# A changed order of eight MLP steps, and two splits queued behind a relu, in a fused attention and MLP kernel

## The chip, the core and the metric

The kernel runs as one program on one NeuronCore of a Trainium2 chip. Its time is the device time of one execution in microseconds. The core has five engines that run side by side and meet through semaphores: TensorE (PE, matrix products into PSUM banks), VectorE (DVE), ScalarE (ACT), GpSimd (POOL) and SyncE (SP, which issues the loads and stores). Each engine takes its own instructions strictly in the order in which they were queued, so an instruction that waits holds up all that stand behind it on that engine.

## The reference, cut to what matters

The kernel chains three blocks on a batch of 2 sequences of 768 tokens and 512 channels: an attention with decay, a token and channel mixing block, and a last block in which the change lies:

```
X = np.fft.fft(np.fft.fft(x, axis=1), axis=2)
u = x + np.real(X)
mu = np.mean(u, axis=-1, keepdims=True)
var = np.mean((u - mu) ** 2, axis=-1, keepdims=True)
un = (u - mu) / np.sqrt(var + 1e-06)
out = u + np.maximum(un @ w_ch1, 0.0) @ w_ch2     # 512 -> 2048 -> 512
```

## The kernel before

The last block works on one sequence b at a time, on halves c of 384 tokens, and on tiles f of 128 of the 2048 hidden channels. Every float32 operand is kept as a high and a low part, and each product is three matmuls (lines 138 to 140, `mm3`): high times high, high weights times low data, low weights times high data, in the order of the code.

A plain step is one pair (c, f). Its first product (`first`) is twelve matmuls of 384 columns from the normalised input `un` of that half and the weight `w_a` into a PSUM bank of the pool `ph`, which has two banks. Then the relu: ACT writes the high part of `hid` (line 515), and DVE the low part (line 516). The second product (`second`) is nine matmuls of 512 columns from `hid` and the weight `w_b` into three accumulator banks `ac`. The loop `run` issues in step i the first product of step i, then the second product of step i-1. So a relu has the second product of one step in which to be done; the third matmul of a second product is the first that reads the low part.

The list `todo` has 68 steps. Steps 60 to 67 are the eight last plain steps, all of sequence 1: tiles f = 0 to 3 of both halves. At the end of step 61, PE transposes the last two rows of tiles of sequence 1 (line 939, `pn`), ACT and DVE turn them into the high and low part of `un` of half c = 1 (lines 945 and 946). Nothing of half c = 1 can be multiplied before.

After the plain steps come groups called `seven`: for two hidden tiles and both halves they do seven half products in place of eight, from sums of weights (`w_s`, lines 241 to 244 on DVE) and sums of inputs (`tops`, `input_sums`, lines 599 to 609). The banks are `pa`, `pb` and `pc`, all from the same pool of two. `pa` is finished by the relu `hid_11`, `v` is collected by lines 657 and 661, and line 664 is the last reader of `pb`. In between, the function `between` puts second products of the group before. The input sums of sequence 1 are queued on DVE after step 61; the last of them, `input_sums_last`, overwrites a quarter of `un` of half c = 1 in place (ACT line 618, DVE line 619), so it must wait for the first product of step 67, which reads the old content.

Weights are loaded by SP into one of three `raw` buffers and split: ACT writes the high part (line 280, or 271 for sums), POOL subtracts it from the raw words for the low part (line 281, or 272). The POOL instruction frees the raw buffer for the next load. The weights of tiles 10 and up come as 64-bit words, and ACT (lines 226 and 229) and DVE (lines 249 and 254) make floats of them first. `convert` takes one such job per step; a job is taken only when weight tiles have become free.

The order on PE and SP is that of the code. The order on DVE, ACT and POOL is made by a scheduler from dependencies and its own estimate of times, except where `tc.issue_after(ins)` puts what is queued in it behind `ins` on the engine of `ins`. `urgent` holds the last relu queued on ACT and on DVE.

Of the kernel before, what the change touches and what calls it, by code (L numbers as in the profile page):

```python
# [57 lines left out]
def f32(ap):  # L58
    return ap.bitcast(F32)
# [3 lines left out]
def body(ctx: ExitStack, tc: tile.TileContext, qkv, kT, lam, w_tok1, w_tok2,  # L63
# [37 lines left out]
    urgent = {}  # L101
# [11 lines left out]
    def acc_bank(n):  # L113
        return ps_acc.tile([P, 512], F32, tag="acc", name=n)
# [7 lines left out]
    def big_tile(n, dt=F32):  # L122
        return big_p.tile([P, BIG], dt, tag="big", name=n)

    def half_tile(shape, n, dt=F32):
        return half_p.tile(shape, dt, tag="half", name=n)

    def temp(w, n, dt=F32):
        return t_p.tile([P, 2 * NQ + 2], dt, tag="t", name=n)[:, :w]
# [57 lines left out]
    def load_next():  # L187
        job = next_job()
        if job is None:
            return False  # L190
        kind, key = job
        at_["load"] += 1
        jobs.append(job)
        raw = raw_p.tile([P, 1024], U32, tag="raw", name="raw_" + "_".join(map(str, key)) + kind[0])
        raws[job] = raw
        if key[0] == "dft":
            nc.sync.dma_start(raw.bitcast(F32)[:, :512], dft[key[1]])
        elif kind == "sums":
            for i, k in enumerate(pair_keys(key)):
                nc.sync.dma_start(raw.bitcast(F32)[:, i * 512:(i + 1) * 512], singles[place_of(k)])  # L200
        elif kind == "single":
            nc.sync.dma_start(raw.bitcast(F32)[:, :512], singles[place_of(key)])
        else:
            w = {"t1": lambda: w_tok1[key[1]], "t2": lambda: w_tok2[key[1], key[2]],
                 "a": lambda: (w_ch1, m_ch1)[key[1]][key[2]], "b": lambda: (w_ch2, m_ch2)[key[1]][key[2]]}[key[0]]()
            nc.sync.dma_start(raw[:, :2 * width(key)], w)
        return True
# [179 lines left out]
    def load_qkv(b, hp):  # L387
        t = half_tile([P, 4, S], f"qkv_{b}_{hp}")
        nc.sync.dma_start(t[:, 0, :], qkv[b, hp, :, 0])
        nc.sync.dma_start(t[:, 1:3, :], qkv[b, hp, :, 1:3])  # L390
        pair[b, hp] = t

    def load_kp(b, hp, kp):
        nc.sync.dma_start(kp, kT[b, hp].rearrange("p (c j) -> p c j", j=C))
# [3 lines left out]
    def attention_scores(b, hp, dT, pw, kp):  # L398
        n = f"{b}_{hp}"
        t = pair[b, hp]  # L400
        q, kn, v, qs = (t[:, i, :].rearrange("p (c j) -> p c j", j=C) for i in range(4))
        sts = {}
        st2 = temp(4 * C, f"st2_{n}").rearrange("p (a c j) -> p a c j", a=2, c=2)
        for g, cs in enumerate((range(4), range(4, NC))):
            m = len(cs)
            ps = [(ph_bank, x_bank)[g](f"s_{n}_{g}_{a}") for a in range(2)]
            for i, c in enumerate(cs):
                for a in range(2):
                    r = slice(a * D, (a + 1) * D)
                    nc.tensor.matmul(ps[a][:, i * C:(i + 1) * C], kp[r, c, :], q[r, c, :], start=True, stop=True)  # L410
            for a in range(2):
                st = st2[:, a] if g else temp(4 * C, f"st_{n}_{a}").rearrange("p (c j) -> p c j", c=4)
                tt(out=st, in0=ps[a][:, :m * C].rearrange("p (c j) -> p c j", c=m),
                   in1=dT[:, 2 * hp + a:2 * hp + a + 1, :].to_broadcast([P, m, C]), op=ALU.mult)
                for i, c in enumerate(cs):
                    sts[c, a] = st[:, i, :]
        nc.gpsimd.tensor_tensor(
            out=qs[:, 1:, :], in0=q[:, 1:, :],
            in1=pw[:, hp:hp + 1, :].to_broadcast([P, NC - 1, C]), op=ALU.mult)
        pair[b, hp] = t, sts  # L420
# [193 lines left out]
    def input_sums_last(b, k):  # L614

        t = tops[b, 4][:, k]
        src = cores.pop((b, k))
        nc.scalar.activation(t[:, 0, :], src, AF.Copy)
        tt(out=t[:, 1, :], in0=src, in1=f32(t[:, 0, :]), op=ALU.subtract)
# [73 lines left out]
    def seconds(b, p, starts, ends):  # L693
        f = 2 * p
        return [(b, c, f_, starts and j < 2, ends and j > 1)
                for j, (c, f_) in enumerate(((0, f), (1, f + 1), (0, f + 1), (1, f)))]
# [17 lines left out]
    def units(m, blocks, last_f):  # L714
        return [(m, fs, b, c, f, f == last_f) for fs, b in blocks for c in range(2) for f in fs]
# [242 lines left out]

    todo = units(0, [(G1[0], 0), (G1[0] + G1[1], 1), (G1[1] + G1[2], 0), (G1[3], 0), (G1[2] + G1[3], 1)], 11)
    todo += units(1, [(G1[0] + G1[1], 0)], 15)  # L960
    todo += [(1, None, 1, c, f, False) for c, f in ((0, 0), (0, 1), (1, 0), (1, 1), (0, 2), (1, 2), (0, 3), (1, 3))]


    by_seven = [(b, p, p == first_p, p == ps[-1]) for b, ps, first_p in (
# [41 lines left out]
    with tc.manual_schedule(engines={ENG.SP, ENG.PE}):  # L1006
        dT, pw, kps, bds, skew = attention_setup()

        def load(n):
            load_kp(n // NP, n % NP, kps[n % NP])  # L1010
            load_qkv(n // NP, n % NP)

        load(2)
        skew(6, H)
        load(3)
        for _ in range(3):
            load_next()
        for b in range(B):
            xT[b] = big_tile(f"xT_{b}")[:, :4 * S].rearrange("p (k s) -> p k s", k=4)

        def scores(n):
            attention_scores(n // NP, n % NP, dT, pw, kps[n % NP])

        def states(n):
            attention_states(n // NP, n % NP, dT, pw)

        def result(n):
            attention_out(n // NP, n % NP, bds[n % 2], x_bank if n == 7 else acc_bank)


        warm = acc_bank("warm")

        def keep_warm(n):
            for _ in range(n):
                nc.tensor.transpose(warm[:, :P], ident, ident)

        def constants():
            rawx = temp(P, "rawx")
            nc.sync.dma_start(rawx, dft_x)
            nc.scalar.activation(cx, rawx, AF.Copy)  # L1040

        keep_warm(22)
        acts = {"s": scores, "u": states, "r": result, "l": load, "c": convert, "x": token_in, "h": token_hidden,
                "o": token_out, "m": run, "w": lambda: keep_warm(8), "k": constants}
        for word in EARLY.split():
            acts[word[0]](*(int(i) for i in word[1:]))
        run(54 - step["i"])
        free = big_tile("tops_0", F32R).rearrange("p (j k h s) -> p j k h s", j=2, k=2, h=2)
        half = half_tile([P, 2, 2, 2, HS], "tops_1", F32R)
        free = [free, big_tile("tops_2", F32R).rearrange("p (j k h s) -> p j k h s", j=2, k=2, h=2)]  # L1050
        homes = {1: (free[0][:, 0], free[0][:, 1], half[:, 0]), 0: (free[1][:, 0], free[1][:, 1], half[:, 1])}
        pieces = [input_sums(0, k, homes[0]) for k in range(2)]
        for fn in pieces[0]:
            fn()
            run(1)
        run(62 - step["i"])
        for k in range(2):
            for fn in input_sums(1, k, homes[1]):
                fn()
        run(64 - step["i"])  # L1060
        input_sums_last(0, 0)
        for fn in pieces[1]:
            run(1)
            fn()
        run(len(todo) - step["i"])
        for k in range(2):
            input_sums_last(1, k)
        pend = [(False, lambda: second(todo[-1]))]

        place = {"i": 0}  # L1070

        def between():
            j, i = divmod(place["i"], 4)
            place["i"] += 1
            turns = TURNS_7[j] * (i + 1) // 4 - TURNS_7[j] * i // 4
            ends, fn = pend.pop(0) if pend else (False, lambda: None)
            if ends:
                fn()
            convert(turns)
            if not ends:  # L1080
                fn()

        for j, u in enumerate(by_seven):
            seven(u[0], u[1], between)
            last = j == len(by_seven) - 1
            todo_ = seconds(*u)
            if last:
                for x in (todo_[0], todo_[2]):
                    second_of(*x)
                second_two(todo_[1], todo_[3])  # L1090
            else:
                pend.extend([(x[4], lambda x=x: second_of(*x)) for x in todo_])
            if j == 0:
                input_sums_last(0, 1)
# [99 lines left out]
```

## Time and profile before

| | us |
|---|---|
| median of 3 runs | 611.98 |
| lowest and highest | 611.23, 612.0 |
| the profiled execution | 612.37 |
| its span, first to last instruction | 610.6 |

The profile comes from one execution. A row of a timeline gives the start in us from the span's beginning, the duration, the engine, the source line, the operation, what it writes and reads, and in brackets the idle time of the engine before it with the instruction that ended it. Names in the timeline have no buffer numbers, so the place of a row is found by its time: step 62 begins at 403.11, the first `seven` at 429.57.

### The profile page before, as it was taken

The numbers are of one execution on the slowest core, as the hardware profiler recorded it, in microseconds if no ns is written. First come the engines' busy times: TensorE is split into PE (matmuls) and PEld (weight loads), VectorE is DVE, ScalarE is ACT, GpSimd is POOL, SyncE is SP. The second block draws the span as 40 slices with busy tenths as digits, with TensorE's granted clock in tenths as the row PEclk, the third lists the DMA queues.
The fourth block names the chain that finished last, engine by engine and source line by source line (L and its number), as shares of the span: only waits on it lengthen the run. The fifth ranks groups of instructions, "written<-read, shape, count | busy, mean of one in ns | idle before, by whom it ended". The sixth has DMA issues, their size and how long they took to land. (4 is left out here: it accounts for less than half of the span.)

```text
span 610.6 us, 9592 instructions
## 1 busy us (share of the span) xinstructions
PE 587.5 (96%) x3704; PEld 546.0 (89%) x3704; DVE 409.9 (67%) x768; ACT 270.3 (44%) x536; POOL 141.8 (23%) x119
## 2 busy tenths in 40 slices
PE   8789999999999999899999999999999999999997
PEld 7677899999999989899989899879888888998886
DVE  6798893474586636938796896798684477443435
ACT  2576971255565554534453461335552453211110
POOL 5253230023240040201364110034420342200000
PEclk9999999999999999999999999999999999999999
DMA  7965341024447764600132000002343132000005
GB/s 278 406 250 206 131 139 41 0 74 135 154 158 244 262 189 145 240 5 2 53 95 78 19 2 34 18 1 86 139 155 105 34 122 87 1 1 0 1 1 206
DMA packets 24637, 65.58 MB, mean 107 GB/s; under 512 B 2824, under 2 KB 3984, under 8 KB 24592
## 3 DMA queue, kind: packets, MB, share of 16 engines
q1 hardware_dynamic: 24304, 64.83, 31.2%
q8 instruction: 29, 0.48, 0.3%
q10 hardware_dynamic: 288, 0.14, 0.1%
q14 instruction: 16, 0.13, 0.1%
HBM read 54.99 MB, written 9.97 MB: 106 GB/s over the span
## 5 line engine op out<-in xcount | busy, mean ns | idle before, releaser
L140 PE MATMUL ac<-w_b,hid 128*128 128x512 f32 x192 | 75.9, 395 | 0.3 <-DVE hid L516 0.3
L516 DVE SCALAR_TENSOR_TENSOR hid<-ph,hid 128x384 fp32r<-128x384 f32 x68 | 37.6, 553 | 56.8 <-ACT hid L515 56.7
L139 PE MATMUL ac<-w_b,hid 128*128 128x512 f32 x192 | 75.7, 394 | 0.0
L138 PE MATMUL ac<-w_b,hid 128*128 128x512 f32 x192 | 74.9, 390 | 0.0
L138 PE MATMUL ac<-hid,w_b 128*128 128x384 f32 x192 | 64.7, 337 | 2.5 <-DVE xT L524 1.9
L139 PE MATMUL ac<-hid,w_b 128*128 128x384 f32 x192 | 64.7, 337 | 1.1 <-DVE hid L516 0.9
L138 PE MATMUL ph<-uh,w_a 128*128 128x384 f32 x192 | 64.7, 337 | 0.4 <-DVE hid L516 0.4
L140 PE MATMUL ac<-hid,w_b 128*128 128x384 f32 x192 | 64.3, 335 | 0.0
L140 PE MATMUL ph<-uh,w_a 128*128 128x384 f32 x192 | 64.2, 335 | 0.0
L139 PE MATMUL ph<-uh,w_a 128*128 128x384 f32 x192 | 64.2, 334 | 0.0
L515 ACT ACTIVATE hid<-ph 128x384 fp32r<-128x384 f32 x68 | 33.1, 486 | 66.0 <-PE ph L140 65.8
L281 POOL TENSOR_TENSOR w_a<-m_a,w_a 128x512 fp32r<-128x512 f32 x18 | 26.3, 1462 | 104.3 <-ACT w_a L280 104.3
L140 PEld LDWEIGHTS ac<-w_b,hid 128*128 128x128 f32 x192 | 36.0, 187 | 8.4 <-DVE hid L516 0.7
L139 PEld LDWEIGHTS ac<-w_b,hid 128*128 128x128 f32 x192 | 36.0, 188 | 6.1
L138 PEld LDWEIGHTS ac<-w_b,hid 128*128 128x128 f32 x192 | 36.1, 188 | 5.8
L138 PEld LDWEIGHTS ac<-hid,w_b 128*128 128x128 f32 x192 | 36.1, 188 | 3.1 <-issue 2.2
L139 PEld LDWEIGHTS ac<-hid,w_b 128*128 128x128 f32 x192 | 36.0, 188 | 2.2 <-DVE hid L516 2.0
L281 POOL TENSOR_TENSOR w_b<-m_b,w_b 128x512 fp32r<-128x512 f32 x18 | 24.4, 1356 | 58.4 <-ACT w_b L280 27.7
L138 PEld LDWEIGHTS ph<-uh,w_a 128*128 128x128 f32 x192 | 36.1, 188 | 0.9 <-DVE hid L516 0.6
L139 PEld LDWEIGHTS ph<-uh,w_a 128*128 128x128 f32 x192 | 36.1, 188 | 0.1
L140 PEld LDWEIGHTS ac<-hid,w_b 128*128 128x128 f32 x192 | 36.0, 188 | 0.0
L140 PEld LDWEIGHTS ph<-uh,w_a 128*128 128x128 f32 x192 | 36.0, 188 | 0.0
(504 smaller groups left out, 1475.9 us busy)
## 6 DMA issues: line engine op xcount, KB each, us to landing
qkv<-qkv SPq DMA_DIRECT2D x7, 768.0 KB, 8.6
single_scratch<-m_a SPq DMA_DIRECT2D x16, 256.0 KB, 4.4
qkv<-qkv SPq DMA_DIRECT2D x10, 384.0 KB, 5.9
kp<-kT SPq DMA_DIRECT2D x8, 384.0 KB, 6.5
out<-u SPq DMA_DIRECT2D x11, 256.0 KB, 2.0
single_scratch<-m_b SPq DMA_DIRECT2D x10, 256.0 KB, 5.4
raw_t_0d<-w_tok SPq DMA_DIRECT2D x2, 384.0 KB, 9.2
raw_t_1d<-w_tok SPq DMA_DIRECT2D x2, 384.0 KB, 3.5
```

Of the source, the lines that this page charges most:

```text
L138: nc.tensor.matmul(ps, wt[0], xt[0], start=first, stop=False, **kw)
L139: nc.tensor.matmul(ps, wt[0], xt[1], start=False, stop=False, **kw)
L140: nc.tensor.matmul(ps, wt[1], xt[0], start=False, stop=last, **kw)
L281: nc.gpsimd.tensor_tensor(out=t[:, 1, :n], in0=src, in1=f32(t[:, 0, :n]), op=ALU.subtract)
L515: mark("act", nc.scalar.activation(hi, ps, AF.Relu))
L516: mark("dve", stt(out=lo, in0=ps, scalar=0.0, in1=f32(hi), op0=ALU.max, op1=ALU.subtract))
```

## The change

Two edits. The order of the eight last plain steps is changed, and the two calls of `input_sums_last` for sequence 1 are queued behind the last relu on ACT and on DVE.

```
-    todo += [(1, None, 1, c, f, False) for c, f in ((0, 0), (0, 1), (1, 0), (1, 1), (0, 2), (1, 2), (0, 3), (1, 3))]
+    todo += [(1, None, 1, c, f, False) for c, f in ((0, 0), (0, 1), (0, 2), (1, 0), (1, 1), (0, 3), (1, 2), (1, 3))]
...
-        for k in range(2):
-            input_sums_last(1, k)
+        with tc.issue_after(urgent["act"]), tc.issue_after(urgent["dve"]):
+            for k in range(2):
+                input_sums_last(1, k)
```

Step 62 is now tile 2 of half 0 instead of tile 0 of half 1; steps 63 to 66 move accordingly, step 67 stays (1, 3). The weights of tiles 0, 1 and 2 are used for the last time one step later than before, and with them the jobs of `convert` that wait for room move back.

On DVE the relu of step 62 stands among the input sums. This is the difference there (`hid_1_0_2` is sequence 1, half 0, tile 2; `x_1_0` and `x_1_1` are input sums of sequence 1):

```order
 L603 TENSOR_TENSOR x_1_0_4309<-x_1_0_4309,x_1_0_4303 128x384
-L599 TENSOR_TENSOR x_1_1_4323<-un_0_4142 128x384
+L609 TENSOR_TENSOR tops_3829<-x_1_0_4307,tops_3829 128x384
 L603 TENSOR_TENSOR x_1_0_4305<-x_1_0_4305,x_1_0_4309 128x384
 L609 TENSOR_TENSOR tops_3829<-x_1_0_4309,tops_3829 128x384
-L609 TENSOR_TENSOR tops_3829<-x_1_0_4307,tops_3829 128x384
+L599 TENSOR_TENSOR x_1_1_4323<-un_0_4142 128x384
 L599 TENSOR_TENSOR x_1_1_4325<-un_3_4180 128x384
 L599 TENSOR_TENSOR x_1_1_4327<-un_3_4180 128x384
 L603 TENSOR_TENSOR x_1_1_4321<-x_1_1_4325,x_1_1_4321 128x384
-L516 SCALAR_TENSOR_TENSOR hid_1_1_0_4352<-ph_1_1_0_4339,hid_1_1_0_4352 128x384
+L516 SCALAR_TENSOR_TENSOR hid_1_0_2_4352<-ph_1_0_2_4339,hid_1_0_2_4352 128x384
```

The low part of step 62's relu has another tile, and the same number of DVE instructions ahead of it as before.

On ACT around the first `seven`, before (`m_1_2` and `hid_2_11` are copies of the bank `pa`, `raw_a_10d` the load of the words of tile 10):

```order
L618 ACTIVATE un_3_4180<-x_1_0_4305 128x384
L618 ACTIVATE un_3_4180<-x_1_1_4323 128x384
L515 ACTIVATE hid_1_1_3_4516<-ph_1_1_3_4503 128x384
L280 ACTIVATE w_b_8_4677<-raw_b_8s 128x512
L647 ACTIVATE m_1_2_4547<-pa_2_4540 128x384
L226 ACTIVATE m_a_10_4724<-raw_a_10d 128x512
L229 ACTIVATE raw_a_10d<-raw_a_10d,floor_by 128x512
L271 ACTIVATE w_s_4_0_4716<-raw_s_4s 128x512
L515 ACTIVATE hid_2_11_4573<-pa_2_4540 128x384
L271 ACTIVATE w_s_4_1_4719<-raw_s_4s 128x512
```

and now:

```order
L515 ACTIVATE hid_1_1_3_4512<-ph_1_1_3_4499 128x384
L618 ACTIVATE un_3_4180<-x_1_0_4305 128x384
L618 ACTIVATE un_3_4180<-x_1_1_4323 128x384
L280 ACTIVATE w_a_9_4672<-raw_a_9s 128x512
L280 ACTIVATE w_b_8_4707<-raw_b_8s 128x512
L647 ACTIVATE m_1_2_4539<-pa_2_4532 128x384
L271 ACTIVATE w_s_4_0_4735<-raw_s_4s 128x512
L226 ACTIVATE m_a_10_4743<-raw_a_10d 128x512
L515 ACTIVATE hid_2_11_4565<-pa_2_4532 128x384
L271 ACTIVATE w_s_4_1_4738<-raw_s_4s 128x512
L229 ACTIVATE raw_a_10d<-raw_a_10d,floor_by 128x512
```

The relu of step 67 (`hid_1_1_3`) goes ahead of the two line-618 copies; the split of `w_a_9`, which stood ahead of all these, follows them; the line-226 copy stays ahead of `hid_2_11`, and its partner on line 229 falls behind it.

On DVE in the same place, now:

```order
L516 SCALAR_TENSOR_TENSOR hid_1_1_3_4512<-ph_1_1_3_4499,hid_1_1_3_4512 128x384
L619 TENSOR_TENSOR un_3_4180<-x_1_0_4305,un_3_4180 128x384
L619 TENSOR_TENSOR un_3_4180<-x_1_1_4323,un_3_4180 128x384
L241 TENSOR_TENSOR raw_s_4s<-raw_s_4s 128x256
L242 TENSOR_TENSOR raw_s_4s<-raw_s_4s 128x256
L243 TENSOR_TENSOR raw_s_4s<-raw_s_4s 128x256
L244 TENSOR_TENSOR raw_s_4s<-raw_s_4s 128x256
L651 TENSOR_TENSOR u_1_2_4548<-pb_2_4541,m_1_2_4539 128x384
L516 SCALAR_TENSOR_TENSOR hid_2_11_4565<-pa_2_4532,hid_2_11_4565 128x384
L657 TENSOR_TENSOR v_1_2_4574<-pb_2_4541,m_1_2_4539 128x384
L249 SCALAR_TENSOR_TENSOR m_a_10_4743<-m_a_10_4743,raw_a_10d 128x512
L661 TENSOR_TENSOR v_1_2_4574<-pc_2_4584,v_1_2_4574 128x384
```

Before, lines 241 to 244 and both of line 619 stood ahead of `hid_1_1_3`, and lines 249 and 254 ahead of `hid_2_11`. Line 249 now stands between lines 657 and 661, and line 254 between lines 661 and 664.

## Rows read from the trace of the kernel before

**Rows 1.** Windows: length, busy us of PE, PEld, DVE, ACT, POOL, granted clock, DMA.

```profile
402.00:430.00 28.00, 26.55 (x133) 23.36 (x132) 25.13 (x43) 13.52 (x27) 12.51 (x7) 1.00 0.19 57
442.00:606.00 164.00, 164.00 (x808) 146.50 (x809) 89.53 (x154) 47.89 (x89) 24.71 (x18) 1.00 0.18 62
```

**Rows 2.** Timeline of PE: transposes before a first product, at step 59 and 62.

```profile
386.09 1.08 PE L939 MATMUL pn<-ident,unf 128*128 128x128 f32 x8 [0.40 <-DVE unf L930]
...
387.36 0.34 PE L140 MATMUL ph<-un,w_a 128*128 128x384 f32 x1
...
401.34 1.04 PE L939 MATMUL pn<-ident,unf 128*128 128x128 f32 x8
403.11 0.44 PE L138 MATMUL ph<-un,w_a 128*128 128x384 f32 x1 [0.74 <-ACT un L945]
...
404.23 0.33 PE L140 MATMUL ph<-un,w_a 128*128 128x384 f32 x1
```

**Rows 3.** Timeline of PE: second product of step 62, second and third matmul.

```profile
410.40 0.40 PE L139 MATMUL ac<-w_b,hid 128*128 128x512 f32 x1
411.11 0.50 PE L140 MATMUL ac<-w_b,hid 128*128 128x512 f32 x1 [0.31 <-DVE hid L516]
```

**Rows 4.** Timeline of DVE, steps 62 to 64.

```profile
402.61 1.29 DVE L946 TENSOR_TENSOR un<-pn,un 128x512 fp32r<-128x512 f32 x2 [1.37 <-ACT un L945]
403.93 1.03 DVE L599 TENSOR_TENSOR x<-un 128x384 f32<-128x384 f32 x2
...
410.50 0.55 DVE L516 SCALAR_TENSOR_TENSOR hid<-ph,hid 128x384 fp32r<-128x384 f32 x1
410.97 1.18 DVE L603 TENSOR_TENSOR x<-x,x 128x384 f32<-128x384 f32 x1
...
414.58 2.11 DVE L609 TENSOR_TENSOR tops<-x,tops 128x384 fp32r<-128x384 f32 x2
```

**Rows 5.** Timeline of POOL, 402 to 441.

```profile
407.27 4.46 POOL L281 TENSOR_TENSOR w_b<-raw_b_6s,w_b 128x512 fp32r<-128x512 f32 x1 [21.61 <-ACT w_b L280]
...
414.87 1.40 POOL L272 TENSOR_TENSOR w_s<-raw_s_3s,w_s 128x512 fp32r<-128x512 f32 x1 [1.57 <-ACT w_s L271]
...
428.84 1.29 POOL L281 TENSOR_TENSOR w_b<-raw_b_8s,w_b 128x512 fp32r<-128x512 f32 x1 [1.26 <-ACT w_b L280]
436.08 2.74 POOL L272 TENSOR_TENSOR w_s<-raw_s_4s,w_s 128x512 fp32r<-128x512 f32 x2 [5.96 <-issue]
439.64 1.29 POOL L281 TENSOR_TENSOR w_b<-raw_b_9s,w_b 128x512 fp32r<-128x512 f32 x1 [0.82 <-DVE v L661]
```

**Rows 6.** Timeline of PE, first seven: last of pa, first of pb, pc, next pa.

```profile
430.45 0.34 PE L140 MATMUL pa<-un,w_a 128*128 128x384 f32 x1
431.86 0.44 PE L138 MATMUL pb<-tops,w_s 128*128 128x384 f32 x1 [1.07 <-DVE hid L516]
...
437.52 0.44 PE L138 MATMUL pc<-tops,w_s 128*128 128x384 f32 x1
...
440.77 0.33 PE L138 MATMUL pa<-un,w_a 128*128 128x384 f32 x1
```

**Rows 7.** Timeline of DVE, first seven.

```profile
430.33 1.01 DVE L619 TENSOR_TENSOR un<-x,un 128x384 fp32r<-128x384 f32 x2
431.26 0.55 DVE L516 SCALAR_TENSOR_TENSOR hid<-ph,hid 128x384 fp32r<-128x384 f32 x1
...
438.88 0.56 DVE L661 TENSOR_TENSOR v<-pc,v 128x384 f32<-128x384 f32 x1 [0.90 <-PE pc L140]
439.93 0.56 DVE L664 TENSOR_TENSOR m<-pb,m 128x384 f32<-128x384 f32 x1 [0.49 <-PE pb L140]
```

**Rows 8.** Timeline of ACT: relu of step 67, line 226, relu of pa.

```profile
427.75 0.49 ACT L515 ACTIVATE hid<-ph 128x384 fp32r<-128x384 f32 x1 [0.57 <-PE ph L140]
...
433.44 0.68 ACT L226 ACTIVATE m_a<-raw_a_10d 128x512 f32<-128x512 f32 x1 [2.06 <-DMA raw_a_10d<-m_ch]
...
436.38 0.49 ACT L515 ACTIVATE hid<-pa 128x384 fp32r<-128x384 f32 x1 [0.43 <-PE pa L140]
```

## The prediction

> **What bounds the kernel now.** I read the windows first, then TensorE's own timeline where it waits, then the engines that it waits for. From 442 to 606 us TensorE is busy all the time, at a granted clock of 1.00; from 402 to 430 it is idle for 1.45 of 28 us [rows 1]. So whatever TensorE loses or wins before 442 arrives at the end undiminished, and no other engine's busy time matters unless TensorE waits for it. The reader should look for TensorE's idle brackets near the change. There are three.
>
> The first is at step 62. The transposes of the last rows start at 401.34, and the first product that reads them has its third matmul at 404.23, which is 2.89 us. Where the input lay ready, at step 59, the same distance was 1.27 [rows 2]. So 1.62 us are lost.
>
> The second is in the second product of step 62: the third matmul, the first that reads the low part of the relu, follows 0.71 after the second [rows 3]. Undisturbed, 512-column matmuls start 0.23 apart: from 404.23 to 410.40 lie 22 steps of 384 columns and 10 of 512, and at 0.175 for the former (18 of them in 3.25, with one restart, from pc to the next pa [rows 6]) the latter come to 0.23. So 0.48 are lost.
>
> The third is in the first seven. The bank pb could have been started 0.17 after 430.45, at 430.62, and was started at 431.86 [rows 6]: 1.24 lost. It waited for the low part of step 67's relu, which DVE took at 431.26, behind the two line-619 splits [rows 7].
>
> The relevant view of DVE is its timeline from 402 to 411: it has no gap. Two evictions from 402.61, then 14 instructions of 0.47 each from 403.93, then the relu of step 62 at 410.50, since 403.93 + 14 x 0.47 = 410.51 [rows 4].
>
> **The change part by part. Edit one, the step order.** The first product of step 62 now reads half 0, which has been ready for long. The wait after the transposes goes: TensorE is 1.62 us earlier. What is late next is the relu of that step. Its ACT half is no obstacle, since it now stands ahead of the input sums' copies. Its DVE half still stands behind the same two evictions and 14 input sums, and these start when the transposes are done, which the edit doesn't move. None of them waits for TensorE after that. So the low part is still written from 410.50 to 411.05 [rows 4], and the third matmul of the second product still starts at 411.11 [rows 3]. The second matmul comes at 410.40 - 1.62 = 408.78, and the wait behind it grows from 0.48 by the same 1.62, to 2.10. Sum of edit one at 411.11: zero.
>
> The next relu, step 63, falls behind six more input sums. It would be taken at about 411.7 (the end of a POOL subtraction, see below) + 6 x 0.47 = 414.5 and be done at 415.1. TensorE needs it after the rest of this second product, the next first product and two matmuls more, at 411.11 + 0.1 + 7 x 0.23 + 12 x 0.175 + 2 x 0.23 = 415.4. It just holds, and I take 0. From there the relus have a step of slack, and TensorE stands at the first seven where it stood before, at 430.45.
>
> The weight splits that wait for room move back by one step. Nothing of them is used before the second seven, after 440.77 [rows 6], so as work they are hidden; what they do to the queues is edit two's matter. On SP the loads of w_a_9, w_b_8, w_s_4 and tile 10 follow their buffers and come later with them; the first that an engine on TensorE's way waits for is tile 10's, below.
>
> **Edit two, the relu of step 67 ahead of the splits.** ACT has the relu at 427.75 to 428.24 as before [rows 8]. On DVE it no longer stands behind lines 241 to 244 and 619, so it can follow at once and end before 429. That is ahead of 430.62, and the 1.24 us are won there.
>
> What is late next is the bank pc, which needs the relu of pa off its bank. Before, this relu started on ACT at 436.38 [rows 8] and pc at 437.52 [rows 6], 1.14 later. ACT takes line 226 ahead of that relu, and line 226 waits for the load of raw_a_10d. Before, the load was freed when POOL ended the split of w_b_8 at 428.84 + 1.29 = 430.13 [rows 5], and line 226 started at 433.44, 3.31 later, long before the relu was ready. Now the ACT copies for w_a_9 and w_b_8 come after the relu of step 67 and the two line-618 copies. Three pieces of the relu's 0.49 each, started 0.4 apart, from 427.75 (an estimate from [rows 8]) and one wider one put the copy of w_a_9 at about 429.0 to 429.7. POOL then needs 1.29 for w_a_9 and 1.29 for w_b_8: 432.3 at the earliest, 433.1 when DVE's weight sums get in between. Plus 3.31, line 226 starts between 435.6 and 436.4. It holds ACT for some 0.6, and behind it stand pa's relu, the second split of w_s_4 and line 229; so the relu of pa starts at 436.2 to 437.0, where 435.1 would have been possible (430.62, then 6 matmuls of pb, 9 of a second product and 6 of pa: 430.62 + 1.05 + 2.09 + 1.05 = 434.8, and 0.3 for the result). So pc starts at 437.35 to 438.15, against 437.52: between -0.2 and +0.6. I take +0.1. The 1.24 won at pb are spent waiting at pc.
>
> Behind pc comes a new cost. Call the start of pa's relu on ACT H (436.38 before). POOL's second split of w_s_4 ended at 436.08 + 2.74 = 438.82 [rows 5], H + 2.44. Line 249 now stands ahead of line 661 on DVE. An instruction of DVE that reads two tiles in SBUF is held while POOL is in a subtraction: the line-603 sum after the relu at 410.97 took 1.18 in place of 0.55 and ended 0.42 after POOL's did at 411.73 [rows 4, 5]. Line 249 is of that kind. It starts at H + 2.44 and takes 0.7, so line 661 starts at H + 3.05 rather than H + 2.50 [rows 7]. Then line 254, ahead of line 664, meets POOL's split of w_b_9, H + 3.26 to H + 4.55 [rows 5], and ends at H + 5.2. Line 664 then ends at about H + 5.7 and the next pa starts at H + 5.8. Before, that was 440.77, H + 4.39 [rows 6]. Cost 1.4, or 0.4 if line 254 gets in ahead of POOL. I take 1.0, towards the upper end, since POOL's request is there first.
>
> The sum is 0 + 0.1 + 1.0 = +1.1 us. The profiled execution took 612.37, so 613.5; the median of the runs lies 0.4 below that execution, which makes 613.1.
>
> The two-tile rule has a page: the Trainium skill, "SBUF — State Buffer", section "Who interferes with whom", says that a DVE instruction with two SBUF inputs and a GpSimd instruction that reads SBUF exclude each other, and that issue order decides who is blocked. The rows agree on the exclusion. On the order they go both ways: a POOL subtraction issued at 407.27 ran only after 410.4 (it ended at 411.73 and takes 1.29), behind seven DVE instructions issued later, and one issued at 414.87 got in after a single DVE instruction, which made the pair of line 609 last 2.11 [rows 4, 5]. By the page's order alone the split of w_b_6, which POOL will now ask for at some 409.6, would go ahead of step 62's relu; that is the second rival below.
>
> **The rivals.** *One: faster.* The load of raw_a_10d is back before pa's relu is ready, at 435.1. Then pc starts at 436.2, which is 1.3 earlier than before, and line 249 is through before POOL's split, so the 1.0 goes as well: 612.37 - 1.3 - 0.4 = 610.7. It needs POOL to end both splits by 431.8. Against it: the first can't start before 429.7.
>
> *Two: slower.* POOL gets SBUF for the split of w_b_6 at the end of a DVE sum near 410.0, ahead of step 62's relu. That pushes the relu, and TensorE's third matmul, from 411.11 by up to 1.2, and everything behind it: 613.1 + 1.2 = 614.3. It decides the case if POOL starts before 410.4. POOL asks for it when ACT has the relu of step 63 and the copy of w_b_6: the first product of step 63 starts its last matmul two before 408.78, at 408.3, its result is there 0.34 later, and 0.4 and 0.6 on ACT make 409.6. For it speaks the split issued at 414.87, against it the one issued at 407.27 [rows 5].
>
> *Three: edit one keeps its gain,* because the DVE relu of step 62 comes out earlier than 410.5 for a reason that the rows don't show: 613.1 - 1.6 = 611.5. The gapless DVE stretch speaks against it.
>
> *Four: the clock.* The wait of 2.1 us at 411 is longer than any of TensorE's here, and the granted clock could fall to 1.2 GHz behind it. A step of 12 x 0.175 + 9 x 0.23 = 4.2 us would take 8.4: +4.2, 617.3. Against it: the clock stays at 1.00 through the stretch with the first two waits [rows 1]. The Trainium skill, "TensorE: Matmul & The Clock Gate", section "What's actually happening", states that an idle TensorE is gated to 1.2 GHz; no wait in this trace shows it.
>
> **How the numbers follow.** My forecast has 60%, rival one 12%, two 18%, three 6%, four 4%. The forecast's own range, from the bounds of its terms (-0.2 to +0.6 at pc, 0.4 to 1.4 behind it), is +0.2 to +2.0: 612.2 to 614.0. A measurement of this kernel can tell a difference of about 0.2%, here 1.2 us. So of the forecast's 60%, 40 are within that and 20 slower. With rival three, within 0.2% has 46%; slower has 20 + 18 + 4 = 42%; faster has 12%. The range runs from 611.0, which takes in most of rival three and the slow end of rival one, to 614.4, which takes in rival two.
>
> **What would show it.** No idle time before the first product of step 62, and a wait of some 2.1 us for the DVE relu before a third matmul at 411.1. No wait at pb at 430.6. ACT idle before line 226 for a load, pa's relu directly behind it, and a wait of TensorE before pc of nearly 2 us. Line 664 behind line 254, and the next pa waiting for it. I am wrong if step 62's relu is taken on DVE well before 410.5, or if line 226 starts before 435.

## The result, and the profile after

The changed kernel took 615.35 us, the median of 12 runs (613.74 to 617.74), and the kernel before took 612.81 on the same chip (12 runs, 611.23 to 614.66). The ratio is 1.0051, with a 95% interval of 1.0035 to 1.0066: slower by 3.1 us (2.1 to 4.0); the two medians alone differ by 2.5. The change was forecast at 613.1 with a range to 614.4, so the result lies beyond the range, on the slow side. The profiled execution took 616.64, with a span of 614.7.

I read the windows first, as before. The columns are length, busy us of PE, PEld, DVE, ACT, POOL, granted clock, DMA.

```profile
402.00:430.00 28.00, 26.00 (x126) 23.30 (x125) 22.76 (x39) 11.91 (x24) 7.72 (x5) 0.94 0.16 41
411.00:416.00 5.00, 4.73 (x16) 4.17 (x17) 5.00 (x11) 1.36 (x3) 0.89 (x1) 0.66 0.23 56
442.00:606.00 164.00, 163.01 (x806) 145.57 (x806) 92.37 (x157) 50.74 (x94) 26.51 (x19) 1.00 0.19 65
```

The granted clock is what is new: 0.94 in the first window, where it was 1.00 [rows 1], and 0.66 from 411 to 416. TensorE's timeline shows where it falls.

```profile
401.51 1.04 PE L939 MATMUL pn<-ident,unf 128*128 128x128 f32 x8
402.30 0.42 PE L138 MATMUL ph<-un,w_a 128*128 128x384 f32 x1
...
408.88 0.40 PE L139 MATMUL ac<-w_b,hid 128*128 128x512 f32 x1
411.27 0.50 PE L140 MATMUL ac<-w_b,hid 128*128 128x512 f32 x1 [2.00 <-DVE hid L516]
411.61 0.41 PE L138 MATMUL ac<-w_b,hid 128*128 128x512 f32 x1
411.84 0.61 PE L139 MATMUL ac<-w_b,hid 128*128 128x512 f32 x1
412.25 0.63 PE L140 MATMUL ac<-w_b,hid 128*128 128x512 f32 x1
...
413.96 0.52 PE L138 MATMUL ph<-un,w_a 128*128 128x384 f32 x1
...
415.24 0.36 PE L139 MATMUL ph<-un,w_a 128*128 128x384 f32 x1
415.44 0.33 PE L140 MATMUL ph<-un,w_a 128*128 128x384 f32 x1
```

The wait after the transposes is gone: the first product starts 0.79 behind them, without idle time. In its place stands the wait of 2.00 for the low part of step 62's relu, and the third matmul starts at 411.27. This timeline was 0.17 later than the old one already at 401.34, so that is 411.10, where it was 411.11 [rows 2, 3]. From 411.84 on 512-column matmuls start 0.41 to 0.43 apart in place of 0.23, which is the lower of the two clock levels (1.2 in place of 2.4 GHz), until 415.3. The window from 411 to 416 has 0.34 x 5 = 1.7 us less of full clock. From 411.84 to 415.24 lie five steps of 512 columns and four of 384, 3.40 us; at 0.23 and 0.175 they would have taken 1.85. So the half clock cost 1.55.

On DVE and POOL the order was as foreseen. The relu still comes behind all the input sums, at 410.67, and POOL's split of `w_b_6`, recorded from 410.00 and 1.89 long in place of 1.29, did not push it:

```profile
410.67 0.55 DVE L516 SCALAR_TENSOR_TENSOR hid<-ph,hid 128x384 fp32r<-128x384 f32 x1
411.14 1.17 DVE L603 TENSOR_TENSOR x<-x,x 128x384 f32<-128x384 f32 x1
```

```profile
410.00 1.89 POOL L281 TENSOR_TENSOR w_b<-raw_b_6s,w_b 128x512 fp32r<-128x512 f32 x1 [24.16 <-ACT w_b L280]
```

Now the first seven. From the timeline of all engines, the chain from the relu of step 67 to the relu of `pa` (it answers to [rows 5, 8]):

```profile
429.49 0.49 ACT L515 ACTIVATE hid<-ph 128x384 fp32r<-128x384 f32 x1 [3.17 <-PE ph L140]
...
430.02 0.56 DVE L516 SCALAR_TENSOR_TENSOR hid<-ph,hid 128x384 fp32r<-128x384 f32 x1 [3.44 <-ACT hid L515]
...
430.71 0.62 ACT L280 ACTIVATE w_a<-raw_a_9s 128x512 fp32r<-128x512 f32 x1
...
431.40 1.59 POOL L281 TENSOR_TENSOR w_a<-raw_a_9s,w_a 128x512 fp32r<-128x512 f32 x1 [3.73 <-ACT w_a L280]
...
432.95 1.47 POOL L281 TENSOR_TENSOR w_b<-raw_b_8s,w_b 128x512 fp32r<-128x512 f32 x1
...
434.45 0.33 SPq L206 DMA_DIRECT2D raw_a_10d<-m_ch  x1
...
438.63 0.66 ACT L226 ACTIVATE m_a<-raw_a_10d 128x512 f32<-128x512 f32 x1 [2.29 <-DMA raw_a_10d<-m_ch]
439.19 0.48 ACT L515 ACTIVATE hid<-pa 128x384 fp32r<-128x384 f32 x1
```

The reader should see three things. The relu of step 67 is done on DVE by 430.6, so `pb` does not wait (1.24 won). The copy of `w_a_9` stands behind it, and POOL ends both splits at 434.42. And from the load's issue to line 226 it is 4.18, where the forecast took 3.31, with pa's relu right behind. It also shares its time with the load ahead of it: `raw_b_9s` is issued at 433.02 and takes 2.7, so it lands at 435.7. In the kernel before that load was issued at 427.61, took 2.5, and was back when raw_a_10d was issued at 430.15. TensorE and DVE then, answering to [rows 6, 7]:

```profile
440.31 0.44 PE L138 MATMUL pc<-tops,w_s 128*128 128x384 f32 x1 [2.54 <-DVE hid L516]
444.81 0.44 PE L138 MATMUL pa<-un,w_a 128*128 128x384 f32 x1 [0.79 <-DVE m L664]
```

```profile
440.87 1.29 DVE L249 SCALAR_TENSOR_TENSOR m_a<-m_a,raw_a_10d 128x512 uint32<-128x512 uint32 x1
442.08 0.55 DVE L661 TENSOR_TENSOR v<-pc,v 128x384 f32<-128x384 f32 x1
442.55 1.73 DVE L254 SCALAR_TENSOR_TENSOR m_a<-raw_a_10d,m_a 128x512 uint32<-128x512 uint32 x1
444.21 0.55 DVE L664 TENSOR_TENSOR m<-pb,m 128x384 f32<-128x384 f32 x1
```

`pc` waits 2.54, and from `pc` to the next `pa` it is 4.50 in place of 3.25, since lines 249 and 254, held up by POOL, stand ahead of lines 661 and 664. They take 1.29 and 1.73; in the kernel before they took 0.69 each:

```profile
434.79 0.69 DVE L249 SCALAR_TENSOR_TENSOR m_a<-m_a,raw_a_10d 128x512 uint32<-128x512 uint32 x1 [0.92 <-ACT raw_a_10d L229]
435.51 0.69 DVE L254 SCALAR_TENSOR_TENSOR m_a<-raw_a_10d,m_a 128x512 uint32<-128x512 uint32 x1
```

The span grew by 4.1: 0.2 ahead of step 62, 0 at the third matmul, 1.55 by the clock, -1.3 at `pb`, 2.4 at `pc`, 1.25 behind it, and small ones.

### The profile page after: what moved, and what is told of

Its sections match the earlier page's. It is cut to its first block, busy times and chain, and to the rows that moved or that the text cites. A ratio compares the mean times of both kernels' runs of the same rounds, so it can differ in the third digit from the quotient of the medians.

```text
span 614.7 us, 9596 instructions
## 1 busy us (share of the span) xinstructions
PE 588.7 (96%) x3704; PEld 547.1 (89%) x3704; DVE 413.0 (67%) x768; ACT 270.1 (44%) x536; POOL 138.9 (23%) x119
```

## The experiments

Theory T: the forecast's chain is right, and what it lacked is the half clock behind the 2.0 us wait and a longer load. Its rivals are named in the expectations. One measure needs a word. The same instructions, from the start to the transposes before step 62, end at 397.9 to 403.2 us in the profiles, so I compare profiles by the stretch from the first transpose of step 62 to the last instruction. All kernels in one table ("clock": the clock halved during or behind a wait inside the stretch; "pc": TensorE's wait before the first seven's `pc`; "load": from the issue of raw_a_10d to line 226, where line 226 waited for it):

| kernel | ratio to before, 95% | stretch | clock | pc | load |
|---|---|---|---|---|---|
| before; once more | 1; 0.9997 [0.9976, 1.0018] | 209.2; 209.1 | no; no | 0; 0 | 3.3; 3.1 |
| changed | 1.0051 [1.0035, 1.0066] | 213.2 | yes | 2.5 | 4.2 |
| changed once more | 1.0050 [1.0031, 1.0069] | 212.7 | yes | 2.1 | 3.7 |
| order alone | 1.0016 [0.9997, 1.0036] | 209.9 | no | 1.0 | 3.3 |
| splits alone | 1.0019 [0.9999, 1.0039] | 210.7 | no | 1.9 | 3.3 |
| changed, sums behind relus | 0.9999 [0.9978, 1.0020] | 210.7 | yes | 2.4 | 4.2 |
| changed, wait filled | 1.0018 [1.0000, 1.0036] | 210.4 | no | 1.6 | 3.2 |
| changed, words behind | 1.0014 [0.9991, 1.0038] | 210.9 | yes | 0.2 | - |
| order, four parts | 1.0010 [0.9993, 1.0027] | 210.1 | no | 0.5 | - |
| order, four parts, words | 0.9998 [0.9979, 1.0016] | 209.3 | no | 0 | - |
| both, five parts, words | 0.9984 [0.9960, 1.0008] | 208.5 | no | 0 | - |
| splits, words behind | 1.0006 [0.9982, 1.0030] | 209.0 | no | 0.2 | - |
| both, sums late | 1.0042 [1.0019, 1.0065] | 212.0 | yes | 3.7 | - |

**The changed kernel once more.** No edit.

> The changed kernel once more, with nothing altered, to see what of its time repeats. Theory T: the wait of 2.0 us before the third matmul of step 62's second product and the order of line 226 and pa's relu on ACT are of the program and come again; the half clock behind the wait and the load time of raw_a_10d (3.2 to 3.3, or 4.2) are of the execution. So the stretch from the first transpose of step 62 to the end lies between 210.6 (neither) and 213.2 (both). Rival R2a: the half clock always follows this wait in this program, and the edit alone that moved the order only escaped it by its other start; then it is there again.

The wait, the half clock and the order on ACT came again:

```profile
409.87 0.79 PE L140 MATMUL ac<-w_b,hid 128*128 128x512 f32 x1 [1.99 <-DVE hid L516]
410.46 0.63 PE L138 MATMUL ac<-w_b,hid 128*128 128x512 f32 x1
```

The 0.79 and 0.63 show the lower clock again. The stretch is 212.7, inside T's bounds. This profile doesn't exclude R2a, but the timed executions do: a stretch like this one takes 1.7 of 613 us, 0.0028, off the mean granted clock, and two of the 24 executions of this program (615.06 and 612.35 us) had a mean of 1.000.

**Order alone** (edit one, without `issue_after`).

> The kernel before with edit one alone, the step order. Theory T: the damage of the change belongs to the order. The 1.7 us won before step 62 come back as a wait of about 2.0 us for the low part of its relu, TensorE's clock is granted at half for some 3.4 us behind that wait (cost 1.5), and the weight jobs, a step later, make line 226 hold ACT until about 438.6, so that pc waits; the wait at pb (1.24) stays too, but as pc's start is set by the load and not by TensorE, it is paid only once. So about as slow as the changed kernel: +2 to +3 us against before, 1.003 to 1.005. Rival R1: the damage belongs to edit two (the relu of step 67 ahead of the splits delays the weight copies on ACT); then the order alone costs only what the clock does, 0 to +1.5 us, and line 226 starts before 437. Rival R2: the half clock is chance and follows no wait; then no stretch below 1.00 directly behind the wait at 411.

T expected 2 to 3 us and got 1.0 (-0.2 to 2.2). The wait is the same, but here the clock did not fall behind it:

```profile
407.61 0.50 PE L140 MATMUL ac<-w_b,hid 128*128 128x512 f32 x1 [1.99 <-DVE hid L516]
407.94 0.40 PE L138 MATMUL ac<-w_b,hid 128*128 128x512 f32 x1
408.18 0.39 PE L139 MATMUL ac<-w_b,hid 128*128 128x512 f32 x1
```

So R2 had this run right. But in the 14 profiles the clock fell five times between 400 us and the end of the sevens, and each time during a wait of TensorE of 1.9 or more or within 1.4 us behind one, never elsewhere. There were nine such waits. So in these profiles the half clock came only with such a wait, and not with each. `pb` started without a wait, against T: lines 241 to 244 come later with their jobs, and no longer stand ahead of the relu. The order alone takes away the wait that the forecast gave to edit two. R1's number fits: 1.0 lies in its 0 to 1.5, and line 226 starts at 431.82, which is 435.3 on the time of the profile before. Its reason doesn't: at a full clock the stretch is still 0.7 longer, and it is lost behind `pc`, from which the next `pa` comes 4.47 later, in place of 3.25. On ACT the copy of `w_a_9` starts 0.39 after the last relu and not 1.22 as above; that is 0.83 of the 1.56 that `pc` waits less; the load, 3.3 and not 4.2, is the other large part:

```profile
424.25 0.49 ACT L515 ACTIVATE hid<-ph 128x384 fp32r<-128x384 f32 x1 [0.57 <-PE ph L140]
424.64 0.62 ACT L280 ACTIVATE w_a<-raw_a_9s 128x512 fp32r<-128x512 f32 x1
```

**Splits alone** (edit two on the old order).

> The kernel before with edit two alone, the two splits behind the last relu. Theory T: the wait at pb goes (-1.24), and because the weight jobs keep their old places the load of raw_a_10d is back by 433.5 as before, so that nothing is given back at pc: -0.8 to -1.4 us against before, 0.998 to 0.9985, the granted clock 1.00 from 402 to 440. Rival R1: the relu ahead of the copies delays line 226, pc waits by what pb won or more: 0 to +1.5 us.

T was wrong here, and R1 nearer: 1.2 us slower (-0.1 to 2.4, so not shown in the times alone), the stretch 1.5 longer. The wait of 1.07 at `pb` is gone, 1.9 is waited before `pc`, and 0.71 more before a later `pc`, at 468.14. ACT:

```profile
429.56 0.49 ACT L515 ACTIVATE hid<-ph 128x384 fp32r<-128x384 f32 x1 [1.53 <-PE ph L140]
429.95 0.93 ACT L618 ACTIVATE un<-x 128x384 fp32r<-128x384 f32 x2
430.77 0.62 ACT L280 ACTIVATE w_b<-raw_b_8s 128x512 fp32r<-128x512 f32 x1
...
436.09 0.68 ACT L226 ACTIVATE m_a<-raw_a_10d 128x512 f32<-128x512 f32 x1 [2.90 <-DMA raw_a_10d<-m_ch]
```

The copy of `w_b_8` now follows the two line-618 copies, 1.21 after the relu's start; before, even POOL's split behind that copy started only 1.09 after it [rows 5, 8]. So the load of raw_a_10d is issued at 432.80, in place of 430.15 on a timeline that runs 1.81 earlier: 0.84 later.

**The wait filled.** Eight matmuls more in the wait, whose results nobody reads:

```
+ for n in range(8):
+     nc.tensor.matmul(extra, t[:, 0, s_], w[:, 0, :], start=n == 0, stop=n == 7)
```

> The changed kernel with eight more 512-column matmuls, into a bank that nobody reads, between the second and the third matmul of step 62's second product. They take 8 x 0.23 = 1.84 us of the 2.0 us in which TensorE waits, and their result is not used. Theory T: the third matmul still starts at about 411.3, but the clock stays at 1.00 behind it: 1.5 us less than the changed kernel in the profile (about 615), in the medians 1 to 1.5. Rival R2 (the clock does not follow the wait): the half clock is still there, and the time is that of the changed kernel, 0 to +0.2.

```profile
406.91 0.40 PE L691 MATMUL ac<-w_b,hid 128*128 128x512 f32 x1
407.14 2.01 PE L693 MATMUL extra<-w_b,hid 128*128 128x512 f32 x8
409.30 0.50 PE L694 MATMUL ac<-w_b,hid 128*128 128x512 f32 x1
409.63 0.40 PE L138 MATMUL ac<-w_b,hid 128*128 128x512 f32 x1
```

TensorE has more work, and the kernel is 2.0 us less slow than the changed one (1.0018 against 1.0050; by the intervals some 0.7 to 3.3). The third matmul is where it was: this timeline runs 1.81 ahead of the one before (its transposes start at 399.53, not 401.34), and 409.30 + 1.81 = 411.11. The clock stays full in this profile, as T expected and R2 did not. But one profile does not show that the filling kept it full, since the order alone had the unfilled wait and a full clock; and the mean clock of the 12 executions, 0.9961, is only 0.0013 above that of the changed kernel. This is also the forecast's own case, full clock and a load of 3.2: `pc` starts at 435.79 + 1.81 = 437.60, the forecast had 437.6, and the stretch is 1.15 longer than before, the forecast's sum was 1.1.

**The sums behind the relus.**

```
- run(62 - step["i"])
+ run(62 - step["i"])
  for k in range(2):
+     run(1)
      for fn in input_sums(1, k, homes[1]):
-         fn()
+         with tc.issue_after(urgent["dve"]):
+             fn()
```

> The changed kernel, with the input sums of sequence 1 queued on DVE in two parts, one behind the relu of step 62 and one behind that of step 63. Theory T: the low part of step 62's relu comes right behind the two evictions, near 406.5; TensorE does not wait before the third matmul, and as it does not wait, the clock stays at 1.00: 2.0 + 1.5 us less there, 0.5 at most given back at step 64, whose relu stands behind 22 sums. 3.0 to 3.5 us less than the changed kernel in the profile, about 613 (in the medians 2 to 3.5 less, since not every run need have the same clock), the waits at pc and behind it as in the changed kernel. Rival R2 (the clock falls for another reason): 2.0 less, and a stretch at half clock is still there. Rival R3 (the wait only moves to step 63 or 64): less than 1 us won.

The ratio is 0.9999: 3.1 us less than the changed kernel, the size that T gave. R3 falls. In its profile the 2.0 us wait is gone and step 64's relu came in time. But step 65's, behind ten more sums that POOL's subtractions stretched, came late, and 1.2 was waited there, more than the 0.5 at most:

```profile
421.43 0.54 DVE L516 SCALAR_TENSOR_TENSOR hid<-ph,hid 128x384 fp32r<-128x384 f32 x1
```

```profile
422.03 0.50 PE L140 MATMUL ac<-w_b,hid 128*128 128x512 f32 x1 [1.23 <-DVE hid L516]
```

The clock fell to half behind the wait at `pc` (2.4) instead, so the stretch is 2.5 less, and not 3.0 to 3.5. A half clock is still there, as R2 had it, but it left the place where the wait had been and appeared behind another wait.

**Tile 10's words behind pa's relu.** Lines 226 and 229 in `issue_after` of that relu.

> The changed kernel with the two ACT copies of tile 10's words (lines 226 and 229) queued behind pa's relu of the first seven. Measured in the profile from the first transpose of step 62 to the last instruction, since executions of one program differ by several us ahead of it: 209.2 before, 213.2 in the changed kernel. Theory T (pc waits because ACT waits for the load of raw_a_10d ahead of pa's relu): the wait before pc falls from 2.7 to 0.3 or less, but lines 249 and 254 on DVE, ahead of lines 661 and 664, now wait for the copies, and the next pa takes part of it back: 1 to 2 us less than the changed kernel at the same clock and load time (211.2 to 212.2 with a half clock behind the wait at 411, 209.7 to 210.7 without). Rival R4 (the load itself or pb's bank holds pc, not the place of line 226 on ACT): the wait before pc stays over 1.5.

```profile
438.42 0.49 ACT L515 ACTIVATE hid<-pa 128x384 fp32r<-128x384 f32 x1 [0.49 <-PE pa L140]
439.33 0.66 ACT L226 ACTIVATE m_a<-raw_a_10d 128x512 f32<-128x512 f32 x1
```

The relu follows its product, and the wait before `pc` falls from 2.5 to 0.2. R4 falls: the place of line 226 on ACT held `pc`. The stretch, 210.9, lies 0.3 under what T gave for a profile with a half clock, since no more than in the changed kernel was waited at the next `pa` (0.8).

**Splits, with the words behind.** The same edit on "splits alone".

> The kernel before with edit two, and lines 226 and 229 of tile 10 behind pa's relu on ACT. Theory T (edit two wins its 1.24 at pb, and loses it only because the copy of w_b_8, now behind the relu and the two line-618 copies, delays tile 10's load, for which ACT waits ahead of pa's relu): the wait before pc falls from 2.1 in the kernel with edit two alone to 0.3, and at most 1 comes back at the next pa or pb; the stretch from the first transpose of step 62 to the end 207.6 to 209.0, that is 0.2 to 1.6 us less than before. Rival R4 (pc waits for something else): the wait stays at 1.5 or more and the stretch at 210 or more.

The wait before `pc` falls from 1.9 to 0.2 and the stretch from 210.7 to 209.0, at the upper end of T's range: most of what `pb` wins, the next `pa` takes (0.8; line 664 is behind line 254 there, which POOL stretched to 1.71). Even so edit two is worth only 0.2, and not shown in the times.

**A better order.** Four kernels tried to keep the gains: edit one with the sums in four parts; the same with tile 10's words behind pa's relu on ACT and behind line 664 on DVE as well; both edits with five parts and tile 10 behind lines 515 and 668 (a line or two further down in that kernel's own rows); and the last sums later still.

> Edit one without edit two, and the input sums queued on DVE in four parts, each behind the relu of a step from 62 to 66 (7 to 8 instructions between two relus). Theory T: no wait over 0.4 in steps 62 to 67, so no half clock there; pc still waits for tile 10's words, 1.1 to 2 us (the load takes 3.3 or 4.2), and the next pa 0.9. The stretch from the first transpose of step 62 to the end: 207.5 to 209, that is 0.2 to 1.7 us less than before. Rival R3 (what is won at step 62 is always given back at pc, since the chain of weight copies is set by POOL and the load and not by TensorE): pc waits over 3 us and the stretch is 209.2 or more.

> As the kernel with the sums in four parts, and tile 10's words behind the work that TensorE waits for: lines 226 and 229 behind pa's relu on ACT, lines 249 and 254 behind line 664 on DVE. Theory T: none of the waits at step 62, pb, pc or the next pa is over 0.4; the stretch from the first transpose of step 62 to the end is 205.8 to 206.8, 2.4 to 3.4 us less than before, the ratio to before 0.9945 to 0.996. Rival R5 (tile 10 then comes too late for the fifth seven, which uses it): a wait of over 1 us before a later pa, and 207.5 or more.

> Both edits, with what the runs so far point to: the input sums of both sequences in five parts, behind the relus of steps 62 to 66, so that none stands behind the last relu; lines 226 and 229 of tile 10 behind pa's relu on ACT, lines 249 and 254 behind the last reader of pc (line 668) on DVE. Theory T: no wait of TensorE over 0.4 from step 62 to the second seven; the stretch from the first transpose of step 62 to the end 205.4 to 206.6 against 209.2 before, so 2.6 to 3.8 us faster, ratio 0.994 to 0.996. Rival R5 (a third resource, DVE with POOL's subtractions between, is the bound in this stretch, and each wait taken away comes back at the next buffer): waits of together over 2 us between 425 and 447, the stretch over 208.5.

> As the kernel with the sums in five parts and tile 10 behind lines 515 and 668, with two more instructions groups moved: the parts of sequence 0's sums and its line 619, of which nothing is used in the first two sevens, go behind line 651 of the first seven instead of ahead of the relu of step 67, and lines 249 and 254 of w_b_10 behind the relu of the second seven's pa. Theory T (the waits that were left, 0.66 and 0.53 at pb and 1.34 at the second seven's pc, are each one relu or eviction behind such instructions on DVE): they go, no other wait over 0.4 comes, and the stretch from the first transpose of step 62 to the end is 205.8 to 207.0 against 209.1 to 209.2 before, 2.2 to 3.4 us faster, ratio 0.9945 to 0.9965. Rival R5 (DVE and POOL together are the bound of this stretch, and waits only change place): the stretch stays at 208 or more.

T's stretch was too short in all four. In the first two the rivals had the length and not the reason: `pc` waited 0.5 and not over 3, and no `pa` behind the first seven waited over 1. In the last two R5 was nearer. Each took away most of the waits that it aimed at, and others came: in the first two, `pb` waited 0.7 for the last relu and 1.3 for line 651, behind the sums' parts that now stood there. The third is the best of all, 0.9984 [0.9960, 1.0008], but not shown to beat before; its new wait, 1.17 before the second seven's `pc`, is DVE's relu behind two word instructions that POOL's subtractions (3.00 from 443.44) held up:

```profile
444.05 1.24 DVE L249 SCALAR_TENSOR_TENSOR m_b<-m_b,raw_b_10d 128x512 uint32<-128x512 uint32 x1 [0.57 <-ACT raw_b_10d L229]
445.33 1.66 DVE L254 SCALAR_TENSOR_TENSOR m_b<-raw_b_10d,m_b 128x512 uint32<-128x512 uint32 x1
446.91 0.55 DVE L517 SCALAR_TENSOR_TENSOR hid<-pa,hid 128x384 fp32r<-128x384 f32 x1
```

The fourth moved five sums behind line 651, and the scheduler put all five ahead of pa's relu. `pc` waited 3.66, and the clock fell again:

```profile
432.69 2.57 DVE L610 TENSOR_TENSOR tops<-x,tops 128x384 fp32r<-128x384 f32 x3
435.18 2.09 DVE L620 TENSOR_TENSOR un<-x,un 128x384 fp32r<-128x384 f32 x2
437.20 0.55 DVE L517 SCALAR_TENSOR_TENSOR hid<-pa,hid 128x384 fp32r<-128x384 f32 x1
```

**Before once more.** No edit.

> The kernel before once more, with nothing altered, for a second profile of it. Theory T: ahead of step 62 its timeline may be moved by up to some 3 us either way, as in the other executions of the same instructions; from the first transpose of step 62 to the end it takes 209.2 again, within 0.3, with the waits of 1.6, 0.5 and 1.2 us where they were, unless the clock is halved behind one of them (then 1.3 to 1.6 more). Rival R6 (the stretch itself is different in each execution by 1 us or more, so that single profiles say nothing of effects of 1 us): under 208.6 or over 209.9 at a clock of 1.00.

The stretch is 209.1, against 209.2, with the same waits. R6 is not borne out by these two profiles, which at the full clock agree to 0.1; the two of the changed kernel, 213.2 and 212.7, differ by as much as their loads. Ahead of it, this execution shows what the first one did not, in two windows of it:

```profile
240.00:246.00 6.00, 4.10 (x25) 3.81 (x24) 4.35 (x8) 2.90 (x5) 0.00 (x0) 1.00 0.41 97
246.00:250.00 4.00, 4.00 (x15) 4.00 (x16) 3.12 (x6) 2.81 (x6) 2.24 (x2) 0.57 1.01 379
```

```profile
245.92 0.41 PE L138 MATMUL ac<-hid,w_b 128*128 128x384 f32 x1 [1.90 <-DVE xT L524]
```

Behind a wait of 1.90 the clock is 0.57 for 4 us, in the kernel before. In the profile that the prediction had, the same wait is 1.93, at 245.24, and the clock stays at 1.00.

## Why the prediction was wrong

**Edit one, zero at 411.11.** Right to 0.01, and so is its reason: the relu's place behind the input sums. Rival two (POOL ahead of that relu) did not come. The Trainium skill, "SBUF — State Buffer", section "Who interferes with whom", lets issue order decide who blocks. Here DVE's queue went on past POOL's request of 410.00, as it had past the one of 407.27 [rows 5].

**Rival four, the clock, was the step that failed.** The sum had no term for it. It had 4% and came in the profile, and in the second one of the same program. Two things in the argument were wrong. "The clock stays at 1.00 through the stretch with the first two waits" was no evidence on a wait of 2.1, since the losses there were 1.6 and 0.5. The one wait of that size in the trace, 1.93 at 245, was passed over. It would have spoken against the rival, since the clock stayed at 1.00 behind it; only the second profile of the same kernel shows it halved there, so one trace could not have given the chance. And the price was taken as a whole step at half speed, 4.2, where it was 1.55.

The Trainium skill, "TensorE: Matmul & The Clock Gate", section "What's actually happening", states that an idle TensorE is gated to 1.2 GHz. Of the four profiles with an unfilled wait of 2.0 in this place, three show that level behind it, and one does not.

In the timed executions the mean granted clock was 0.9948 for the changed kernel (24 executions) and 0.9971 for before (116). What these 0.0023 cost can only be estimated. In the profile 0.0028 of the mean cost 1.55, which makes 1.3 us. Within the kernels, over all 272 timed executions, 0.001 less of mean clock went with 0.32 us more, which makes 0.7. So the clock is a third to two thirds of the 2.0 that the forecast lacked.

**Edit two, 1.24 at pb.** Won, but edit one alone wins it too. I took the cause from the `issue_after`, and didn't ask where lines 241 to 244 stand without it.

**pc, +0.1.** It held in the profile with a full clock and a load of 3.2 (437.60). In the profile of the changed kernel the load took 4.18, and `pc` came 440.31 - 437.52 = 2.8 later than before; of these 0.17 + 1.55 were already there, so that the term was +1.1, 0.5 over its upper end. The term was sized by one row of one execution, 3.31; in the eight profiles in which line 226 waited for it, the load took 3.1 to 3.3 in five, 3.7 in one and 4.2 in two. Why is open, but it need not be chance alone: the three long ones are all among the four of these eight in which `raw_b_9s` was issued only 1.3 to 1.4 ahead (the fourth took 3.2); where it was 1.9 to 3.4 ahead, the load took 3.1 to 3.3. No run moves the two loads apart. That the copy of `w_a_9` would come later was in the forecast.

**Behind pc, +1.0.** It was 1.25, within its bounds, by the mechanism named: lines 249 and 254.

So the sum of the forecast, 1.1, is what the kernel costs in the profile at a full clock, the one with the wait filled (1.15; in that kernel's times 1.1, from 0 to 2.2). The rest of the 3.1 is the clock, by the estimates 0.7 to 1.3, and the load, up to 0.9 if it is as long in the timed executions as in the profile; how long it is there no run shows. Against the forecast's 613.1 the base counts too: the kernel before was taken at 612.0 from 3 runs, and came to 612.81 in 12.

What isn't settled is how often a wait of some 2 us brings the half clock. The order alone has the same wait, and the mean clock of its 12 executions, 0.9970, is not below that of before (these means count every stretch at half clock in an execution, those ahead of step 62 too). The changed kernel has two such waits, the second before `pc`, and either may bring it. With the first of them alone, in the kernel with tile 10's words behind pa's relu, the mean is 0.9962; with the second alone, in splits alone, 0.9954; with a wait of 3.7, in "both, sums late", 0.9928; and in "both, five parts, words", with no wait over 1.2 there, 0.9983.

## What to carry to other kernels

A wait that is only moved isn't worth the same in its new place: losses of 1.6 and 0.5 made one wait of 2.0, and behind that the clock fell in three of four profiles. Before a relu is put ahead of copies, ask which load those copies free, and who on the same engine will wait for that load ahead of the next relu. Price a load from several executions, and ask which other load the change puts beside it. Measure effects of 1 us over a stretch that begins behind the part that varies.

## What was not expected of the hardware

- The kernel with more work was faster: eight matmuls in a wait of 2.0 us, 2.0 us less (1.0018 against 1.0050 to 1.0051). That the clock did it is not shown: 0.0013 more of mean clock is an estimated 0.4 to 0.7 us.
- Behind waits of 1.9 to 2.5 us the half clock came in some executions (at 246, 411 and 438) and not in others of the same instructions. What decides it is not shown.
- The same instructions reach step 62 up to 3.5 us earlier or 1.8 later than in the first profile; most of the differences arise in the first 35 us and at 217 to 250 us. So the time of a single execution does not show an edit of 1 us in this kernel.
